# Half-row projections in one burst, the tails' first MLP layer with stationary weights, and a split last output group in a fused attention and gated-MLP kernel

## The chip, the cores and the metric

The kernel runs on one core of a Trainium2 chip. A core has a matrix engine (TensorE, PE in the profile, with its weight loads shown apart as PEld), three engines that work on tiles in on-chip memory (VectorE or DVE, ScalarE or ACT, GpSimd or POOL), and SyncE (SP), which here only issues transfers. Each engine runs its own instructions in order; semaphores join them. Matrix products land in PSUM, which has eight banks of 2 KB per partition; one bank holds 128 partitions by 512 float32 values. The metric is the device time of one launch in microseconds. The kernel before takes 278.93 us, the median of 13 runs from 277.47 to 279.93.

## The reference

Eight batches of eight heads, 576 tokens, head size 64, go through an attention with a feature map instead of a softmax, and the result through a gated MLP:

```python
def phi(x):                                  # x: q or k, w_phi: 64 x 128
    proj = einsum('bhsd,df->bhsf', x, w_phi)
    proj = proj - max(abs(proj), axis=-1)
    return concatenate([exp(proj), exp(-proj)], axis=-1)
q_p, k_p = phi(q), phi(k)
kv  = einsum('bhsf,bhsd->bhfd', k_p, v)
num = einsum('bhsf,bhfd->bhsd', q_p, kv)
den = einsum('bhsf,bhf->bhs', q_p, k_p.sum(axis=2)) + 1e-06
x = (num / den)                              # laid out as batch, token, 512

h = maximum(x @ w_in, 0)                     # 512 -> 1024
u, v = h[..., :512], h[..., 512:]
v_n = (v - mean(v)) / sqrt(var(v) + 1e-06)
v_s = einsum('ts,bsd->btd', w_spatial, v_n) + b_spatial
out = (u * v_s) @ w_out                      # 512 -> 512
```

## The kernel before, in words

The 576 tokens of a batch are cut into four blocks of 128 and a tail of 64. The attention works in *units*. A pair unit holds two heads of one batch with all four blocks, so eight slots of 128 tokens; a tail unit holds the tails of two neighbouring batches, all eight heads. There are 32 pair units and 4 tail units, 36 in all.

`step(i)` writes out one step of a software pipeline by hand. In each step the units near `i` pass their phases in the order of `ORDER`: keys, queries, attention, sums, next, features, out, maxima; a unit reaches the later phases some steps after the first ones (`LAGS`). The instructions stay on each engine in the order in which they are written. In the phase "keys" `a_keys` (L270) projects the keys: `by_token` (L263) fills one PSUM bank by two matmuls, each with 128 tokens of two heads as stationary operand (128 rows: 64 of one head, 64 of the other) and `wphi2`, a block-diagonal 128x256 copy of `w_phi`, as moving operand. So half the products are with zeros. DVE reduces the bank to the largest absolute value per token and head (L278), and ACT takes two exponentials of it (L281). `a_scale` then scales the values on POOL (L306). The phase "queries" does the same projection of the queries, of which only the maxima are taken (L292), split in a high and a low bfloat16 part (L295, L296), and turned by a PE transpose (`a_max_t`, L327). The phase "features" projects the queries a second time, by feature (L344, L348, L357), with the maxima subtracted by the same matmuls, and ACT takes exponentials (L365). "sums" forms `kv` (L378, L380), "attention" the quotient (L398, L388, L389).

Between the phases, `fill(share)` takes tasks of the MLP from `queue`. Each task has a cost in us of PE time (`MM` for four matmuls of 512 columns, `MS` for five). A step spends `share` of `rate` at each phase, at most `CAP` saved up, and a task is written out once the credit covers half its cost. `b_tasks(b)` (L604) lists the tasks of a batch: the first output groups of the batch before, `b_v_tail` (the v half of the first layer for the 64 tail tokens), four `b_v`, the norms, four `b_u`, `b_u_tail`, four `b_s` (the product with `w_spatial`), `b_s_tail`; the output groups `b_o` are mixed in. What is left when the units are done runs at the end, where `out_tasks(b)` of the last batch closes the kernel: four `b_o` and `b_o_tail`, each a product, a copy out of PSUM by DVE and ACT in turn (L564), and stores from the SP queue (L570, L576).

`b_v_tail` (L488) calls `v_mm` (L444): four matmuls whose stationary operand is `xTt`, 128 rows by 64 tail tokens, and whose moving operand is 512 columns of `w_in` (L447); then ACT's Relu (L449) and DVE's statistics (L450, L451). `b_u_tail` (L519) does the u half the other way round: sixteen matmuls with a 128x128 block of `w_in` stationary and the 64 tokens moving (L527), then one Relu (L529).

All PSUM tiles come from one pool of eight banks, `psum`, which is handed out in turn: a tile waits until the tile taken eight before it has been read. SBUF tiles have pools of their own with fixed numbers of buffers: `vr` five, `ob` six, `uTt` one.

Of the kernel before, what the change touches and what calls it, by code (L numbers as in the profile page):

```python
# [16 lines left out]
def kernel(  # L17
# [15 lines left out]
    nc = tc.nc  # L33
# [6 lines left out]
    P = 128  # L40
# [81 lines left out]

    wphi_f = cpool.tile([P, F], FP32)
    for i in range(2):
# [137 lines left out]

    def by_token(xT, half):  # L263
        ps = psum.tile([P, 4, F], FP32, tag="bank", name="ps")
        for x in range(2):
            nc.tensor.matmul(out=ps[:, 2 * x:2 * x + 2, :], lhsT=xT[:, 2 * half + x, :], rhs=wphi2,  # L266
                             start=True, stop=True)
        return ps

    def a_keys(u):  # L270

        u["mk"] = small.tile([P, H], FP32, tag="mk", name="mk")
        u["kf"] = feat.tile([P, 2, H, F], BF16, tag="kf" if u["pair"] else "kf_t", name="kf",
                            bufs=4 if u["pair"] else 2)
        for half in range(2):
            pk = by_token(u["kT"], half)
            hs = slice(4 * half, 4 * half + 4)
            nc.vector.tensor_reduce(out=u["mk"][:, hs], in_=pk, axis=AX.X, op=ALU.max,  # L278
                                    apply_absolute_value=True)
            for s, sc in ((0, 1.0), (1, -1.0)):  # L280
                nc.scalar.activation(out=u["kf"][:, s, hs, :], in_=pk, func=AF.Exp, bias=0.0, scale=sc)  # L281

    def a_queries(u):

        m, early = mhl[u["i"] % NM], u["i"] < EARLY
        if not early:
            mq = small.tile([P, H], FP32, tag="mq", name="mq")
        for half in range(2):
            pq = by_token(u["qT"], half)
            if early and half == 0:  # L290
                mq = pq[:, 0, 0:H]
            nc.vector.tensor_reduce(out=mq[:, 4 * half:4 * half + 4], in_=pq, axis=AX.X, op=ALU.max,  # L292
                                    apply_absolute_value=True)
        eng = nc.vector if early else nc.gpsimd
        eng.tensor_copy(out=m[:, 0:H], in_=mq)  # L295
        eng.tensor_tensor(out=m[:, H:2 * H], in0=mq, in1=m[:, 0:H], op=ALU.subtract)  # L296

# [211 lines left out]
    def b_u(b, dc):  # L509
# [7 lines left out]
        nc.scalar.activation(out=d["uT"][:, dc, :], in_=pu, func=AF.Relu, bias=0.0, scale=1.0)  # L517

    def b_u_tail(g, bls):  # L519
        d = gs[g]  # L520
        if bls[0] == 0:
            d["uTt"] = s2.tile([P, KC, P], BF16, tag="uTt", name="uTt", bufs=1)
        r = slice(bls[0] * TL, (bls[-1] + 1) * TL)
        pu = psum.tile([P, KC, P], FP32, tag="bank", name="pu")
        for dc in range(KC):
            for kc in range(KC):
                nc.tensor.matmul(out=pu[:, dc, r], lhsT=w_in_bf[:, kc, dc * P:(dc + 1) * P],  # L527
                                 rhs=d["xTt"][:, kc, r], start=(kc == 0), stop=(kc == KC - 1))
        nc.scalar.activation(out=d["uTt"][:, :, r], in_=pu[:, :, r], func=AF.Relu, bias=0.0, scale=1.0)  # L529

# [36 lines left out]
    def b_o(b, j):  # L567
        ob = o_mm(lambda dc: st[b]["uT"][:, dc, j * P:(j + 1) * P], slice(0, P))
        dst = bass.AP(tensor=out.tensor, offset=out.offset + b * S * DM + POS[j] * DM, ap=[[NB * DM, P], [1, DM]])
        nc.sync.dma_start(out=dst, in_=ob)  # L570

    def b_o_tail(g, bls):
        r = slice(bls[0] * TL, (bls[-1] + 1) * TL)
        ob = o_mm(lambda dc: gs[g]["uTt"][:, dc, r], r)
        for bl in bls:
            nc.sync.dma_start(out=out[2 * g + bl, T0:S, :], in_=ob[bl * TL:(bl + 1) * TL, :])  # L576
# [71 lines left out]
    def step(i):  # L648
# [120 lines left out]
```

## Time and profile before

| what | value |
|---|---|
| median of the runs | 278.93 us (13 runs, 277.47 to 279.93) |
| the profiled execution's own time | 279.18 us |
| its span, first to last instruction | 277.4 us |
| PE matmuls | 3047, busy 257.5 us (93%) |
| weight loads | 3047, busy 171.8 us (62%) |
| DVE | 614 instructions, busy 236.8 us (85%) |
| ACT | 501 instructions, busy 218.4 us (79%) |
| POOL | 312 instructions, busy 184.0 us (66%) |
| projections by token, L266 | 288 matmuls of 256 columns |
| units' keys phases | the first at 5.8 us, the last at 221.5 us; 28 of 36 start after 41 us |

A matmul's row in the profile has the time from its start until its result is out, and neighbours overlap; what a matmul takes of PE is the time from its start to the next one's start. A form such as 128\*64 128x512 names the rows and columns of the stationary operand that are in use and then the output's partitions and columns. Idle time of an engine is listed with what ended it. The span ends some us after the last store is issued, when its landing has been seen by SP and the engines have met.

### The profile page before, as it was taken

The page shows a single profiled execution, that of the slowest core. Times are in us where ns is not written, and L with a number is a line of the kernel's source. Part 1 is how long each engine was busy: PE and PEld are TensorE (multiplying, and loading weights), DVE is VectorE, ACT ScalarE, POOL GpSimd, SP SyncE. Part 2 cuts the span into 40 slices and gives each one's busy share as a digit, 9 for nine tenths or more (in the row PEclk, how much of TensorE's full clock was granted, in tenths as well). Part 3 has the DMA queues.
Part 4 walks back from the last instruction along what each step waited for, and adds up shares of the span by engine and source line. Part 5 has one row for each costly group of instructions (what it writes and reads, how often), then busy time and mean ns, then how long its engine had stood idle before and what let it go on. Part 6 is the DMA issues. An engine that isn't in the chain of part 4 may idle for free.

```text
span 277.4 us, 8178 instructions
## 1 busy us (share of the span) xinstructions
PE 257.5 (93%) x3047; PEld 171.8 (62%) x3047; DVE 236.8 (85%) x614; ACT 218.4 (79%) x501; POOL 184.0 (66%) x312
## 2 busy tenths in 40 slices
PE   3858999999999999999998999999998999999993
PEld 2547876767665676666765766667665765554441
DVE  7979998879999989998989989997998897565751
ACT  7898998797888978999898978998798977633511
POOL 4899899999579964898687954998448632410200
PEclk9999999999999999999999999999999999999998
DMA  7999999999999998999989999799854301211115
GB/s 194 201 258 131 158 157 94 158 224 209 184 188 190 231 217 134 224 177 221 132 112 192 258 188 151 167 225 165 140 90 122 87 2 58 94 42 40 76 40 189
DMA packets 84840, 42.43 MB, mean 153 GB/s; under 512 B 51840, under 2 KB 80192, under 8 KB 84800
## 3 DMA queue, kind: packets, MB, share of 16 engines
q1 hardware_dynamic: 60240, 30.95, 52.7%
q0 software_dynamic: 24400, 10.89, 36.9%
q8 instruction: 24, 0.39, 0.6%
q14 instruction: 16, 0.13, 0.2%
q10 hardware_dynamic: 160, 0.07, 0.1%
HBM read 32.85 MB, written 9.44 MB: 152 GB/s over the span
## 4 chain that ended last, share of the span: by engine, by line
PE 72%; ACT 11%; DVE 8%; POOL 3%; issue 2%; DMA 2%; SPq 0%; ACTq 0%
PE pv L447 10%; PE ps L536 10%; PE po L561 9%; PE pu L515 9%; PE ps L266 7%; ACT kf L281 6%; PE pv L378 5%; PE pn L398 4%; ACT qf L365 3%; PE pq L344 3%; PE ps L537 2%; DVE mk L278 2%; DMA first<-in_k_dram 2%; PE pn L426 2%; PE ps L548 1%
## 5 line engine op out<-in xcount | busy, mean ns | idle before, releaser
L306 POOL TENSOR_TENSOR vs<-v_f,em 128x512 bf16<-128x512 f32 x64 | 65.4, 1043 | 27.7 <-ACT em L301 25.2
L281 ACT ACTIVATE kf<-ps 128x512 bf16<-128x512 f32 x144 | 75.3, 633 | 7.4 <-DVE mk L278 7.4
L365 ACT ACTIVATE qf<-pq 128x512 bf16<-128x512 f32 x128 | 66.5, 621 | 10.2 <-PE pq L344 7.5
L278 DVE TENSOR_REDUCE mk<-ps 128x4 f32<-128x512 f32 x72 | 46.3, 681 | 1.0 <-PE ps L266 0.3
L292 DVE TENSOR_REDUCE mq<-ps 128x4 f32<-128x512 f32 x62 | 39.8, 678 | 2.1 <-PE ps L266 2.0
L561 PE MATMUL po<-w_out_bf,uT 128*128 128x512 bf16 x128 | 32.3, 379 | 1.0 <-ACT kf L281 0.8
L461 POOL TENSOR_TENSOR rs<-var,neghalf 64x1 f32<-64x1 f32 (+1 forms) x16 | 12.8, 799 | 30.5 <-DVE var L456 30.2
L536 PE MATMUL ps<-w_spT,vn 128*128 128x512 bf16 x128 | 33.0, 379 | 0.0
L450 DVE BATCH_NORM_STATS2 stats<-vr 128x6 f32<-128x512 bf16 (+1 forms) x40 | 26.7, 684 | 6.5 <-ACT vr L449 6.2
L515 PE MATMUL pu<-xT,w_in_bf 128*128 128x512 bf16 x128 | 32.1, 379 | 0.0
L447 PE MATMUL pv<-w_in_bf,xT 128*128 128x512 bf16 x128 | 31.4, 379 | 0.7 <-ACT kf L281 0.6
L449 ACT ACTIVATE vr<-pv 128x512 bf16<-128x512 f32 (+1 forms) x40 | 23.8, 618 | 8.8 <-PE pv L447 8.4
L539 DVE TENSOR_TENSOR uT<-ps,uT 128x512 bf16<-128x512 f32 x32 | 22.0, 687 | 8.5 <-PE ps L537 7.6
L378 PE MATMUL pv<-vs,kf 128*128 128x66 bf16 x512 | 24.5, 193 | 1.3 <-ACT kf L281 1.2
L389 DVE TENSOR_TENSOR x<-pn,rc 128x256 bf16<-128x256 f32 x64 | 25.0, 416 | 0.3
L398 PEld LDWEIGHTS <-qf 128*128 128x128 bf16 x512 | 20.2, 97 | 7.4 <-issue 1.7
L517 ACT ACTIVATE uT<-pu 128x512 bf16<-128x512 f32 x32 | 19.6, 640 | 6.3 <-PE pu L515 3.2
L378 PEld LDWEIGHTS <-kf 128*128 128x128 bf16 x512 | 21.7, 97 | 4.2 <-issue 3.5
L380 PE MATMUL pv<-vst,kf 128*128 128x66 bf16 x128 | 21.2, 191 | 1.9 <-POOL vst L61 1.9
L398 PE MATMUL pn<-kv,qf 128*128 128x66 bf16 x512 | 21.9, 193 | 0.9 <-ACT kf L281 0.3
L564 ACT COPY ob<-po 128x512 f32<-128x512 f32 x18 | 11.0, 612 | 14.3 <-PE po L561 8.8
L467 POOL TENSOR_SCALAR vn<-vr,rs 128x512 bf16<-128x512 bf16 x28 | 21.3, 769 | 0.9
(130 smaller groups left out, 564.2 us busy)
## 6 DMA issues: line engine op xcount, KB each, us to landing
out_dram<-ob SPq DMA_DIRECT2D x32, 256.0 KB, 2.9
v_f<-in_v_dram SPq DMA_DIRECT2D x14, 512.0 KB, 5.7
k_bf<-in_k_dram POOLq DMA_DIRECT2D x14, 256.0 KB, 6.5
q_bf<-in_q_dram POOLq DMA_DIRECT2D x14, 256.0 KB, 5.9
qt<-qT_b SPq DMA_DIRECT2D x24, 64.0 KB, 4.2
v_tl<-in_v_dram SPq DMA_DIRECT2D x8, 128.0 KB, 5.6
v_f<-in_v_dram SPq DMA_DIRECT2D x1, 1024.0 KB, 9.2
w_in_bf<-in_moe_w_in_dram POOLq DMA_DIRECT2D x2, 512.0 KB, 6.2
```

The lines of the kernel that those rows point to most:

```text
L278: nc.vector.tensor_reduce(out=u["mk"][:, hs], in_=pk, axis=AX.X, op=ALU.max, apply_absolute_value=True)
L281: nc.scalar.activation(out=u["kf"][:, s, hs, :], in_=pk, func=AF.Exp, bias=0.0, scale=sc)
L292: nc.vector.tensor_reduce(out=mq[:, 4 * half:4 * half + 4], in_=pq, axis=AX.X, op=ALU.max, apply_absolute_value=True)
L306: nc.gpsimd.tensor_tensor(out=vs[:, s, :, 0:D], in0=st[u["b"]]["v"][:, pj * H:(pj + 1) * H, :], in1=em[:, s, :].unsqueeze(2).to_broadcast( ...
L365: nc.scalar.activation(out=qf[:, s], in_=pq, func=AF.Exp, bias=0.0, scale=sc)
L378: nc.tensor.matmul(out=pv[:, hh, s, :], lhsT=u["kf"][:, s, 4 * hh + c, :], rhs=u["vs"][:, s, 4 * hh + c, :], start=(c == 0), stop=False)
L398: nc.tensor.matmul(out=pn[:, pos, :], lhsT=u["qf"][hh][:, s, pos, :], rhs=d["kv"][:, 2 * u["pj"] + hh, s, :], start=(s == 0), stop=(s == 1))
L447: nc.tensor.matmul(out=pv[r], lhsT=lhs(kc), rhs=w_in_bf[:, kc, HALF:DFF], start=(kc == 0), stop=(kc == KC - 1))
L450: nc.vector.bn_stats(out=stats[r], in_=dst[r])
L515: nc.tensor.matmul(out=pu, lhsT=w_in_bf[:, kc, dc * P:(dc + 1) * P], rhs=d["xT"][:, kc, :], start=(kc == 0), stop=(kc == KC - 1))
L536: nc.tensor.matmul(out=ps, lhsT=d["vn"][:, sp, cs], rhs=w_spT[:, sp, 0:T0], start=(sp == 0), stop=False)
L561: nc.tensor.matmul(out=po[r], lhsT=lhs(dc), rhs=w_out_bf[:, dc, :], start=(dc == 0), stop=(dc == KC - 1))
```

## The change

- `by_token` now takes a whole unit's keys or queries. For each of the four slots of two heads it issues two matmuls on half of the rows each: rows 0 to 63 (one head) against the first 128 columns of `wphi2`, rows 64 to 127 (the other head) against the last 128. The two heads' results go to two different PSUM banks. So 8 matmuls of 128 columns replace 4 of 256.
- `a_project`, new, does both keys and queries at the start of "keys": 16 matmuls in a row into four banks. The phase "queries" only reads.
- The banks now hold heads of one parity instead of four neighbouring heads; `mk`, `kf` and the two halves of `mhl` are written with a stride of two heads so that all that follows finds its order.
- `b_v_tail` forms both halves of the tail's first layer with `w_in` stationary and 64 tokens moving, 32 matmuls into one bank, and two Relus; `b_u_tail` is gone. `b_turn_tail`, new, runs two `b_v` later: four PE transposes of the v half, a DVE copy, and the statistics. Its cost in the queue is `MM / 4`.
- In the last batch the tail's output group runs second, and the last group, `b_o_last`, is done in two halves of 256 columns, copied by ACT and DVE and stored from ACT's and SP's queues.
- `wphi_f` moves from a buffer of its own into the ring `ob`; `uTt` gets two buffers; `vTt` shares the ring `vr`.

```diff
-    wphi_f = cpool.tile([P, F], FP32)
+    wphi_f = s2.tile([P, F], FP32, tag="ob", name="wphi_f", bufs=6)
...
-    def by_token(xT, half):
-        ps = psum.tile([P, 4, F], FP32, tag="bank", name="ps")
-        for x in range(2):
-            nc.tensor.matmul(out=ps[:, 2 * x:2 * x + 2, :], lhsT=xT[:, 2 * half + x, :], rhs=wphi2,
-                             start=True, stop=True)
+    def by_token(xT):
+        ps = [psum.tile([P, 4, F], FP32, tag="bank", name="ps") for _ in range(2)]
+        for j in range(4):
+            for y in range(2):
+                r = slice(y * D, (y + 1) * D)
+                nc.tensor.matmul(out=ps[y][:, j, :], lhsT=xT[r, j, :], rhs=wphi2[r, y * F:(y + 1) * F],
+                                 start=True, stop=True)
         return ps
+
+    def parity(t, y):
+        return t.rearrange("p (j two) -> p j two", two=2)[:, :, y]
+
+    def a_project(u):
+        u["pk"], u["pq"] = by_token(u["kT"]), by_token(u["qT"])
...
-        for half in range(2):
-            pk = by_token(u["kT"], half)
-            hs = slice(4 * half, 4 * half + 4)
-            nc.vector.tensor_reduce(out=u["mk"][:, hs], in_=pk, axis=AX.X, op=ALU.max,
+        for y, pk in enumerate(u["pk"]):
+            nc.vector.tensor_reduce(out=parity(u["mk"], y), in_=pk, axis=AX.X, op=ALU.max,
                                     apply_absolute_value=True)
             for s, sc in ((0, 1.0), (1, -1.0)):
-                nc.scalar.activation(out=u["kf"][:, s, hs, :], in_=pk, func=AF.Exp, bias=0.0, scale=sc)
+                nc.scalar.activation(out=u["kf"][:, s].rearrange("p (j two) f -> p j two f", two=2)[:, :, y, :],
+                                     in_=pk, func=AF.Exp, bias=0.0, scale=sc)
...
+        for y, pq in enumerate(u["pq"]):
+            nc.vector.tensor_reduce(out=mq[:, 4 * y:4 * y + 4], in_=pq, axis=AX.X, op=ALU.max, apply_absolute_value=True)
...
     def b_v_tail(g, bls):
         d = gs[g]
+        if bls[0] == 0:
+            d["uTt"] = s2.tile([P, KC, P], BF16, tag="uTt", name="uTt", bufs=2)
+        d["vTt"] = s2.tile([P, KC, TL], BF16, tag="vr", name="vTt", bufs=5)
         r = slice(bls[0] * TL, (bls[-1] + 1) * TL)
+        pu = psum.tile([P, 2 * KC, TL], FP32, tag="bank", name="pu")
+        for dc in range(2 * KC):
+            for kc in range(KC):
+                nc.tensor.matmul(out=pu[:, dc, :], lhsT=w_in_bf[:, kc, dc * P:(dc + 1) * P],
+                                 rhs=d["xTt"][:, kc, r], start=(kc == 0), stop=(kc == KC - 1))
+        nc.scalar.activation(out=d["vTt"], in_=pu[:, KC:2 * KC, :], func=AF.Relu, bias=0.0, scale=1.0)
+        nc.scalar.activation(out=d["uTt"][:, :, r], in_=pu[:, 0:KC, :], func=AF.Relu, bias=0.0, scale=1.0)
+
+    def b_turn_tail(g, bls):
+        d = gs[g]
+        r = slice(bls[0] * TL, (bls[-1] + 1) * TL)
+        pt = psum.tile([P, KC, P], BF16, tag="bank", name="pt")
+        for dc in range(KC):
+            nc.tensor.transpose(out=pt[r, dc, :], in_=d["vTt"][:, dc, :], identity=ident)
         vr = s2.tile([P, HALF], BF16, tag="vr", name="vr", bufs=5)
...
-        v_mm(lambda kc: d["xTt"][:, kc, r], vr, r, stats, mv[:, 0, :])
+        nc.vector.tensor_copy(out=vr[r], in_=pt[r].rearrange("p n e -> p (n e)"))
+        nc.vector.bn_stats(out=stats[r], in_=vr[r])
+        nc.vector.bn_aggr(out=mv[r, 0, :], in_=stats[r])
         d["ln"] = vr, moments(mv, r, 1)
...
+    def b_o_last(b, j):
+        dst = bass.AP(tensor=out.tensor, offset=out.offset + b * S * DM + POS[j] * DM, ap=[[NB * DM, P], [1, DM]])
+        for y, copy, queue_ in ((0, nc.scalar.copy, nc.scalar), (1, nc.vector.tensor_copy, nc.sync)):
+            n = slice(y * DM // 2, (y + 1) * DM // 2)
+            po = psum.tile([P, DM // 2], FP32, tag="bank", name="po")
+            for dc in range(KC):
+                nc.tensor.matmul(out=po, lhsT=st[b]["uT"][:, dc, j * P:(j + 1) * P], rhs=w_out_bf[:, dc, n],
+                                 start=(dc == 0), stop=(dc == KC - 1))
+            ob = s2.tile([P, DM], FP32, tag="ob", name="ob", bufs=6)
+            copy(out=ob[:, 0:DM // 2], in_=po)
+            queue_.dma_start(out=dst[:, n], in_=ob[:, 0:DM // 2])
...
+        if b == B - 1:
+            ts = ts[:1] + ts[-1:] + ts[1:NB - 1] + [(MM, lambda: b_o_last(b, NB - 1))]
...
-        ts = outs[:1] + [(MM, lambda: b_v_tail(g, [bl]))] + vs[:2] + outs[1:2] + vs[2:]
+        ts = outs[:1] + [(MM, lambda: b_v_tail(g, [bl]))] + vs[:2]
+        ts += [(MM / 4, lambda: b_turn_tail(g, [bl]))] + outs[1:2] + vs[2:]
...
-        ts += [(MM / 2, lambda: b_u_tail(g, [bl]))] + ss
+        ts += ss
...
                 if what == "keys":
+                    a_project(u)
                     a_keys(u)
```

More of the change, by code (lines that the diff above doesn't have):

```diff
@@ L274, in a_keys @@
                             bufs=4 if u["pair"] else 2)
-        for half in range(2):
-            pk = by_token(u["kT"], half)
-            hs = slice(4 * half, 4 * half + 4)
-            nc.vector.tensor_reduce(out=u["mk"][:, hs], in_=pk, axis=AX.X, op=ALU.max,
+        for y, pk in enumerate(u["pk"]):
+            nc.vector.tensor_reduce(out=parity(u["mk"], y), in_=pk, axis=AX.X, op=ALU.max,
                                     apply_absolute_value=True)
             for s, sc in ((0, 1.0), (1, -1.0)):
-                nc.scalar.activation(out=u["kf"][:, s, hs, :], in_=pk, func=AF.Exp, bias=0.0, scale=sc)
+                nc.scalar.activation(out=u["kf"][:, s].rearrange("p (j two) f -> p j two f", two=2)[:, :, y, :],
+                                     in_=pk, func=AF.Exp, bias=0.0, scale=sc)
     def a_queries(u):
         m, early = mhl[u["i"] % NM], u["i"] < EARLY
-        if not early:
+        if early:
+            mq = u["pq"][0][:, 0, 0:H]
+        else:
             mq = small.tile([P, H], FP32, tag="mq", name="mq")
[L288 to L293, printed above, removed]
+        for y, pq in enumerate(u["pq"]):
+            nc.vector.tensor_reduce(out=mq[:, 4 * y:4 * y + 4], in_=pq, axis=AX.X, op=ALU.max, apply_absolute_value=True)
         eng = nc.vector if early else nc.gpsimd
-        eng.tensor_copy(out=m[:, 0:H], in_=mq)
-        eng.tensor_tensor(out=m[:, H:2 * H], in0=mq, in1=m[:, 0:H], op=ALU.subtract)
+        hi, lo = (m[:, e * H:(e + 1) * H].rearrange("p (j two) -> p two j", two=2) for e in range(2))
+        mq = mq.rearrange("p (two j) -> p two j", two=2)
+        eng.tensor_copy(out=hi, in_=mq)
+        eng.tensor_tensor(out=lo, in0=mq, in1=hi, op=ALU.subtract)
     def a_scale(u):
@@ L517, in b_u @@
         nc.scalar.activation(out=d["uT"][:, dc, :], in_=pu, func=AF.Relu, bias=0.0, scale=1.0)
[L519 to L529, printed above, removed]
     def b_s(b, dc):
```

## The prediction

> **What bounds the kernel now.** I read the page's shares and slices first, then the busy time of two stretches, the waits, and last the timeline around the lines that change.
>
> ```profile
> PE 257.5 (93%) x3047; PEld 171.8 (62%) x3047; DVE 236.8 (85%) x614; ACT 218.4 (79%) x501; POOL 184.0 (66%) x312
> ...
> PE   3858999999999999999998999999998999999993
> ...
> DVE  7979998879999989998989989997998897565751
> ```
> ```profile
> 40.00:230.00 190.00, 185.76 (x2277) 125.75 (x2274) 173.42 (x441) 164.60 (x385) 142.78 (x245) 1.00 1.05 165
> 230.00:277.40 47.40, 42.86 (x374) 22.89 (x373) 27.13 (x72) 19.53 (x37) 7.72 (x13) 0.98 0.23 79
> ```
> ```profile
> DVE uT L539 <- PE ps L537: 4.2, 6, 1.0
> DVE qT_b L330 <- PE pt L327: 4.2, 6, 1.0
> DVE mq L292 <- PE ps L266: 2.0, 5, 0.7
> ```
>
> The second fence holds two stretches: length, then busy time (and instructions) of PE, PEld, DVE, ACT, POOL, then the granted clock, here 1.00. There are three stages. Up to 40 us PE has gaps and is not the bound. From 40 to 230 us PE is busy 185.8 of 190 us and DVE 173.4 (91%), so DVE has 16.6 us to spare; the third fence (waits in that stretch) shows that much of that slack is spent waiting for PE. After 230 us only PE is near full. So PE time saved after 40 us counts, until DVE has no slack.
>
> **The projections.** What the old ones take of PE is read from starts in the timeline, not from the rows' 273 ns:
>
> ```profile
> 120.47 0.60 PE L266 MATMUL ps<-wphi,kT_b 128*128 128x256 bf16 x4
> 120.91 1.03 PE L561 MATMUL po<-w_out_bf,uT 128*128 128x512 bf16 x4
> ```
> ```profile
> 53.88 0.40 PE L236 MATMUL pt<-ident,wsp 128*128 128x128 bf16 x4
> 54.21 0.20 PE L236 MATMUL pt<-ident,wspt 64*128 64x64 bf16 x1
> 54.34 0.41 PE L236 MATMUL pt<-ident,wsp 128*64 128x128 bf16 x8
> 54.68 0.22 PE L236 MATMUL pt<-ident,wspt 64*64 64x64 bf16 x2
> ```
> ```profile
> 133.39 0.28 PE L344 MATMUL pq<-qT_b,wm 128*128 128x128 bf16 x2
> 133.59 0.29 PE L439 MATMUL pt<-ident,xt 64*128 64x64 bf16 x4
> 133.81 0.23 PE L327 MATMUL pt<-ident,mhl 128*128 128x128 bf16 x1
> ```
>
> Four matmuls of 256 columns take 0.44 us, 0.109 each; a unit has eight: **0.872 us**. The new unit has sixteen of 128 columns on half the rows. Does a pair on different rows run together? No row of the trace has that. The nearest is L236 at 54.34, pairs on different *columns* of the array: eight matmuls in 0.34 us, and within it the starts come in pairs, 3 ns inside a pair and mostly 56 ns from pair to pair, which is what one 128-column matmul takes (the L344 rows at 133.39: 56 ns). Sixteen in eight pairs are then 8 x 56 = 0.45 us; the densest stream in the trace (L527 below) has 29 ns per load and matmul, 16 x 29 = **0.464**, which I take. The other end is no overlap: 16 x 56 = 0.90.
>
> Here a rule speaks against the change. The Trainium skill, "TensorEngine Tiling (Array Packing)", Key Properties, says that switching the tiling mode, not just the tile, drains TensorE. The last fence prices it. L439 works on 64 rows. From 133.39 two L344 take 0.11, so it could start at 133.50; it starts at 133.59. Its four take 0.12 (29 each), so L327 could start at 133.71; it starts at 133.81. Each way costs 0.095 us. Had I left the rule out, a unit would save 0.872 - 0.464 = 0.41; with it, in and out once per burst: 0.872 - 0.464 - 0.19 = **0.218 us per unit**. A second rule is harsher: "TensorE: Matmul & The Clock Gate", Back-to-back issue gap, gives about 81 ns sustained for a load and a 128-column matmul; sixteen one after another would be 1.3 us and the unit 0.61 slower. The L344 rows, each with its own load, take 56, so the trace decides against that figure.
>
> 28 units start after 41 us: 28 x 0.218 = 6.1 us. For the eight before I take nothing: from 20 to 40 us DVE is busy 19.3 of 20, and the first bank of keys is complete at 0.095 + 0.45 instead of 0.22, queries earlier than before; either sign stays under 0.5 us in all.
>
> **The tails' first layer**, eight times:
>
> ```profile
> 138.50 1.05 PE L447 MATMUL pv<-w_in_bf,xTt 128*64 128x512 bf16 x4
> 139.48 0.29 PE L344 MATMUL pq<-qt,wm 128*128 128x128 bf16 x2
> ```
> ```profile
> 262.91 0.63 PE L527 MATMUL pu<-xTt,w_in_bf 128*128 128x64 bf16 x16
> 263.37 0.38 PE L536 MATMUL ps<-w_spT,vn 128*128 128x512 bf16 x1
> ```
>
> Old v half: 0.98 us from start to start, the way out included, and 0.09 in: 1.07. New: sixteen with the weights stationary, as L527 has them, 0.46; then the four turns, 64 columns of the array, 4 x 56 and two switches, 0.41; 0.87 together. The u half is 0.46 before and after. Gain 0.2 x 8: 1.2 us in the middle stretch, 0.3 after it. ACT trades a Relu of 64x512 (593 ns) for one of 128x256 (461): 1 us less, not on the path. **DVE gains a copy** of 64x512 out of PSUM, nearest row L413 (128x512, 419 ns): 8 x 0.42 = 3.4 us, 2.5 of it before 230 us. The new wait is the turn on ACT's Relu. Two `b_v` (1.73 us) lie between; an ACT read of a `b_v` bank begins 0.3 us (median) to 1.8 us (one in ten) after PE is done, so rarely late; behind it would wait all of PE, and DVE's statistics. I take nothing, at most 0.3 us x 8.
>
> **The end.**
>
> ```profile
> 271.83 1.03 PE L561 MATMUL po<-w_out_bf,uTt 128*128 128x512 bf16 x4
> ...
> 272.94 0.59 ACT L564 COPY ob<-po 128x512 f32<-128x512 f32 x1 [1.14 <-PE po L561]
> 273.55 1.11 SPq L576 DMA_DIRECT2D out_dram<-ob  x2
> ```
>
> Now: copy 0.59, then two stores; the second issues at 274.07. New: the last half's DVE copy is 128x256, 0.42 by L389, so one SP store issues near 272.95 + 0.42 = 273.37. ACT's half finishes 0.44 us earlier on PE and its store goes from ACT's own queue. The tail's two stores go before. Landing as now: **0.7 us** off. A slower landing from ACT's queue could take it all back.
>
> **Edits at nothing.** `wphi_f` in `ob`: with four `first` and `wspt` it makes six tiles in six buffers, all read long before the first output copy at 75 us. `vTt` in `vr`: the sixth tile takes its buffer, free after the turn. The strides of two heads keep runs of 128 elements. POOL's 31 pairs of L295/L296 keep their sizes. SP keeps its transfers and has one store more at the end, off its queue.
>
> **What takes some back: the banks.** PSUM tiles take the eight banks in turn. I paired every tile in the trace with its last reader. In the 27 units from 48 us on, the tiles taken 4, 3 and 2 before a keys phase are free 0.61, 1.29 and 1.99 us after its start (median), 0.90, 1.66 and 2.58 in the slowest tenth; two of them are the features' banks, read by ACT for 2.06 us:
>
> ```profile
> 139.99 0.60 PE L266 MATMUL ps<-wphi,kT_b 128*128 128x256 bf16 x4
> 140.20 2.06 ACT L365 ACTIVATE qf<-pq 128x512 bf16<-128x512 f32 x4
> ```
>
> The burst takes four banks at once. The next tile comes at 0.65 us (0.095 + 0.464 + 0.095), those behind it at 1.51 and 2.4 with tasks of 0.86: spare 0.04, 0.22 and 0.4 us in the median, short by about 0.2 in the slow tenth. Before, the queries' two banks were asked for only after one or two tasks. Price: 0 to 0.25 us per unit; I take 0.1, near the median: 28 x 0.1 = 2.8 us. This is also how a busier DVE and ACT would hold PE back, so I don't charge DVE again.
>
> **Sum.** Middle: 6.1 + 1.2 - 2.8 = 4.5 us. DVE there: (173.4 + 2.5) of 185.5 us, 95%; from 20 to 40 us it ran at 97%, so it can. Later: 0.3 + 0.7 = 1.0. In all **5.5 us off the span of 277.4: 271.9**. That execution took 279.18 and the median is 278.93; I take the difference from the median: **273.4 us**.
>
> **Rivals.**
> - *All of it arrives.* The burst hands DVE and ACT their work sooner, and the three waits shown above (10.4 us) shrink with PE. No bank stall: 8.3 us off, 270.6. Against it: DVE would be at 175.9 of 182.7, 96%.
> - *DVE and the banks become the bound.* A stall of 0.26 us per unit, the slow tenth everywhere, eats 7.3 us: only the end is left, 277.9; with DVE's 2.5 us uncovered, 280.4. For it: ACT's 2 us of features at each keys phase. Against it: PE waited only some 4 us for readers in this stretch.
> - *The row halves do not overlap* (slower). Place: the burst. 0.90 + 0.19 - 0.872 = +0.214 us per unit, x 28 = +6.0; tails and end give 2.2 back: +3.8, **282.7**. It decides once sixteen matmuls take more than 0.68 us, 43 ns each, before the rest. For it: no pair on rows stands in the trace. Against it: the pairs on columns do overlap, and the two row halves here go to different banks.
>
> **How the numbers follow.** Chances: partial gain 0.45 (own range 271 to 276), all of it 0.20, DVE and banks 0.18, no overlap 0.13, else 0.04. Within 0.2% (0.56 us) is about what a measurement here cannot tell from no change. Faster: 0.45 + 0.20 + 0.07 of the third + 0.01 = 0.73; same 0.06; slower 0.13 + the rest = 0.21. The range 269.8 to 280.6 holds the first two and most of the third case, and leaves the no-overlap case above it.
>
> **What would show it.** Right: matmuls on 64 rows starting in pairs a few ns apart, a burst near 0.46 us with about 0.095 before and behind; PE's busy share still over 95% from 40 to 225 us; DVE near 95% there; few PE waits on L365's and the keys' readers; last SP issue followed by the same landing. Wrong: starts 56 ns apart in the burst; PE waiting for ACT right behind the burst by more than 0.2 us per unit; PE held at the turn; DVE without idle time while PE has gaps.

## The result, and the profile after

The changed kernel takes 281.29 us (median of 11 runs, 280.08 to 282.27) against 278.89 us (48 runs, 277.43 to 280.13): the ratio is 1.009, with a 95% interval of 1.0072 to 1.0107. It is 2.4 us slower, where 5.5 us faster was forecast (273.4 us), and it lies 0.7 us above the top of the stated range, 280.6 us. Its profiled execution took 280.58 us. Below, differences in us are the ratio's distance from 1, times 278.9 us.

The page of the changed kernel, shares and slices:

```profile
span 278.8 us, 9013 instructions
...
PE 252.9 (91%) x3467; PEld 166.8 (60%) x3467; DVE 239.1 (86%) x623; ACT 216.7 (78%) x501; POOL 184.2 (66%) x312
...
PE   3787899899996999999997999999987999999993
...
DVE  7989998969999899998899898997999897565752
```

PE's busy time fell by 4.6 us, and the span still grew by 1.4 us. From the seventh of the 40 slices on (after 40 us) PE's row has slices of 6, 7 and 8; before, all of these but the last were 8 or 9.

The same two stretches as before, length first, then busy time of PE, PEld, DVE, ACT and POOL:

```profile
40.00:230.00 190.00, 179.94 (x2589) 119.59 (x2588) 173.17 (x441) 161.90 (x382) 141.66 (x243) 1.00 1.03 164
230.00:278.80 48.80, 43.63 (x407) 23.89 (x402) 28.59 (x77) 19.46 (x38) 7.71 (x13) 0.98 0.22 77
```

From 40 to 230 us PE is idle for 10.1 us; before it was 4.2. DVE is busy for 173.2 us, as before (173.4): in the same 190 us it did no more than it had done, though the kernel now asks more of it.

The waits of that stretch (who waited, for what: us, times, longest):

```profile
ACT kf L287 <- DVE mk L284: 10.7, 15, 2.3
...
DVE qT_b L337 <- PE pt L334: 4.4, 5, 1.2
...
PE pv L385 <- ACT kf L287: 3.4, 5, 1.4
...
PE ps L268 <- DVE x L396: 2.1, 4, 0.8
...
DVE uT L553 <- PE ps L551: 1.7, 4, 0.4
```

DVE's wait for the product with `w_spatial` (then 4.2 us) has shrunk. What has grown is the chain from DVE to ACT to PE: ACT's exponentials of the keys wait 10.7 us for the key maxima (before 5.0), and PE's sums wait 3.4 us for ACT (before 1.2). A new one is PE's burst waiting for DVE to empty a bank. In the chain of work that ended last, PE had 72% and DVE 8% before; the page of the changed kernel has

```profile
PE 49%; DVE 23%; ACT 10%; DMA 6%; issue 4%; POOL 3%; SPq 3%; POOLq 0%; ACTq 0%
```

These shares alone do not tell a slower kernel from a faster one: the projections alone, which lose nothing, have PE 47% and DVE 18%, and the fastest version below that still computes the reference has PE 46% and DVE 20%.

The timeline around one burst of the changed kernel (start, duration, engine, and what it does):

```profile
127.03 0.22 PE L334 MATMUL pt<-ident,mhl 128*128 128x128 bf16 x1
127.18 0.40 PE L268 MATMUL ps<-wphi,kT_b 64*128 64x128 bf16 x8
127.42 0.39 PE L268 MATMUL ps<-wphi,qT_b 64*128 64x128 bf16 x8
...
127.73 1.04 PE L550 MATMUL ps<-w_spT,vn 128*128 128x512 bf16 x4
```

L334 takes 0.056 us, so PE is free at 127.09 and the burst starts at 127.18: about 0.095 us to switch in. The next matmul starts 0.55 us after the burst began: the burst's 0.46 and about 0.09 to switch out. Inside, starts are 3 to 4 ns apart in a pair and 56 ns from pair to pair. So what the burst itself costs came out as forecast. Another burst did not go so well, in the timeline of the same kernel:

```profile
85.00 0.40 PE L268 MATMUL ps<-wphi,kT_b 64*128 64x128 bf16 x8
85.37 0.38 PE L268 MATMUL ps<-wphi,qT_b 64*128 64x128 bf16 x4
86.11 0.41 DVE L396 TENSOR_TENSOR x<-pn,rc 128x256 bf16<-128x256 f32 x1
86.57 0.38 PE L268 MATMUL ps<-wphi,qT_b 64*128 64x128 bf16 x4 [0.82 <-DVE x L396]
...
88.90 1.29 DVE L284 TENSOR_REDUCE mk<-ps 128x4 f32<-128x512 f32 x2
89.62 2.06 ACT L287 ACTIVATE kf<-ps 128x512 bf16<-128x512 f32 x4 [2.35 <-DVE mk L284]
...
90.76 0.29 PE L385 MATMUL pv<-vs,kf 128*128 128x66 bf16 x4 [1.42 <-ACT kf L287]
```

The burst stops in its middle for 0.82 us, because the bank it needs next still holds what DVE reads at 86.11. Its keys are complete by 85.4, but DVE takes their maxima only at 88.9: until then it works without a gap at what stands ahead in its queue (two blocks' statistics, the quotients, two copies). ACT waits 2.35 us and PE 1.42 us. A faster burst is worth nothing here.

### The profile page after: what moved, and what is told of

Read it like the earlier page. It is cut to its first block, busy times and chain, and to the rows that moved or that the text cites. A ratio compares the mean times of both kernels' runs of the same rounds, so it can differ in the third digit from the quotient of the medians.

```text
span 278.8 us, 9013 instructions
## 1 busy us (share of the span) xinstructions
PE 252.9 (91%) x3467; PEld 166.8 (60%) x3467; DVE 239.1 (86%) x623; ACT 216.7 (78%) x501; POOL 184.2 (66%) x312
## 4 chain that ended last, share of the span: by engine, by line
PE 49%; DVE 23%; ACT 10%; DMA 6%; issue 4%; POOL 3%; SPq 3%; POOLq 0%; ACTq 0%
PE ps L550 8%; PE po L575 7%; PE pu L541 7%; ACT kf L287 6%; PE pv L454 5%; DVE mk L284 4%; DVE stats L457 3%; PE pv L385 3%; PE ps L268 3%; SPq L61 3%; PE pn L405 3%; DMA qT_b<-q_bf 3%; DVE x L396 2%; PE pu L504 2%; PE pq L351 2%
## 5 line engine op out<-in xcount | busy, mean ns | idle before, releaser
L298 DVE TENSOR_REDUCE mq<-ps 128x4 f32<-128x512 f32 x62 | 40.5, 678 | 0.2
L541 PE MATMUL pu<-xT,w_in_bf 128*128 128x512 bf16 x128 | 31.4, 379 | 0.0
L457 DVE BATCH_NORM_STATS2 stats<-vr 128x6 f32<-128x512 bf16 x32 | 21.5, 682 | 8.4 <-ACT vr L456 8.3
L396 DVE TENSOR_TENSOR x<-pn,rc 128x256 bf16<-128x256 f32 x64 | 25.0, 416 | 0.4
L456 ACT ACTIVATE vr<-pv 128x512 bf16<-128x512 f32 x32 | 19.5, 623 | 4.8 <-PE pv L454 4.5
L578 ACT COPY ob<-po 128x512 f32<-128x512 f32 x17 | 10.2, 603 | 16.4 <-PE po L575 16.2
```

Of the source, the lines that this page charges most:

```text
L298: nc.vector.tensor_reduce(out=mq[:, 4 * y:4 * y + 4], in_=pq, axis=AX.X, op=ALU.max, apply_absolute_value=True)
L396: nc.vector.tensor_tensor(out=x, in0=pn[r, :, 0:D], in1=rc[r].to_broadcast([n, 4, D]), op=ALU.mult)
L541: nc.tensor.matmul(out=pu, lhsT=w_in_bf[:, kc, dc * P:(dc + 1) * P], rhs=d["xT"][:, kc, :], start=(kc == 0), stop=(kc == KC - 1))
```

## The experiments

Each ratio is against the kernel before, timed on the same chip. The first four experiments take the change apart.

**The projections alone.**

```diff
-            pk = by_token(u["kT"], half)
...
+    def a_project(u):
+        u["pk"], u["pq"] = by_token(u["kT"]), by_token(u["qT"])
...
+        for y, pk in enumerate(u["pk"]):
```

> The projections alone: half rows, keys and queries in one burst; tails and last group as before. Theory A (the burst asks for four banks at once, while DVE and ACT are behind, and PE stands where it used to run a task): slower than before, by 1 to 3 us (280 to 282). Theory B (the extra DVE copy and the turn of the tails cost the time, the burst is a gain): faster by 1 to 4 us (275 to 278).

Measured: 278.94 us, ratio 0.9998 [0.9974, 1.0022]. Neither theory forecast it: no gain and no loss. The stretch of 40 to 230 us in this kernel:

```profile
40.00:230.00 190.00, 180.48 (x2471) 117.65 (x2502) 173.00 (x441) 164.98 (x387) 143.01 (x245) 1.00 1.09 166
```

By its busy time PE has 5.3 us less to do than before (180.5 against 185.8), and what it saved has become idle time. The 5.3 is somewhat too high: the trace has 2471 matmuls of this stretch for 2502 weight loads, so 31 records are missing. DVE, ACT and POOL have got through as much as before (441, 387 and 245 instructions, then 441, 385 and 245).

**The tails' first layer alone.**

```diff
-        v_mm(lambda kc: d["xTt"][:, kc, r], vr, r, stats, mv[:, 0, :])
...
+        for dc in range(2 * KC):
+            for kc in range(KC):
+                nc.tensor.matmul(out=pu[:, dc, :], lhsT=w_in_bf[:, kc, dc * P:(dc + 1) * P],
+                                 rhs=d["xTt"][:, kc, r], start=(kc == 0), stop=(kc == KC - 1))
...
+        ts += [(MM / 4, lambda: b_turn_tail(g, [bl]))] + outs[1:2] + vs[2:]
```

> The tails' change alone: first layer with stationary weights, v turned back. Theory A: within 0.7 us of before. Theory B: slower by 2 to 4 us (281 to 283), with DVE late in the stretches of the v tasks and about 0.8 us lost before the last w_spatial products.

Measured: 282.27 us, ratio 1.0133 [1.0101, 1.0164], +3.7 us, as theory B forecast. The loss is here. In this kernel's waits the same one has grown, from 5.0 to 9.1 us:

```profile
ACT kf L281 <- DVE mk L278: 9.1, 8, 2.4
```

**The last group alone.**

```diff
+        for y, copy, queue_ in ((0, nc.scalar.copy, nc.scalar), (1, nc.vector.tensor_copy, nc.sync)):
...
+        if b == B - 1:
+            ts = ts[:1] + ts[-1:] + ts[1:NB - 1] + [(MM, lambda: b_o_last(b, NB - 1))]
```

> The last output group alone in two halves, tail's group second. Both theories: 0.2 to 0.7 us faster (the profiles before and after put the time from PE's end to the span's end at 4.5 and 4.3 us).

Measured: 278.76 us, ratio 0.9995 [0.998, 1.0011]. No difference that can be told, where both theories looked for 0.2 to 0.7 us.

**Half rows, but the queries' projection left in its own phase** (two banks at a time, two more mode switches per unit).

```diff
     def a_project(u):
-        u["pk"], u["pq"] = by_token(u["kT"]), by_token(u["qT"])
+        u["pk"] = by_token(u["kT"])
...
+        u["pq"] = by_token(u["qT"])
```

> Half rows, but the queries projected in their own phase as before, so two banks at a time; tails and last group as before. PE then pays the mode switch four times a unit: 0.872 - 0.464 - 0.38 = 0.03 us saved per unit, 1 us in all at most. Theory A: 0 to 1 us faster than before, so 2 to 3 us faster than the projections in one burst. Theory B: 0 to 1 us faster than before, and slower than the burst by 1 to 4 us.

Measured: 279.20 us, 1.0019 [0.9997, 1.0041]. That is level with the burst within the intervals; both theories looked for 0 to 1 us faster than before.

The three parts alone add up to +3.5 us, the whole to +2.5. The next four look at what each costs by itself.

**The burst with the old full rows.**

```diff
+    def a_project(u):
+        u["pk"] = [by_token(u["kT"], half) for half in range(2)]
+        u["pq"] = [by_token(u["qT"], half) for half in range(2)]
```

> The burst without the half rows: keys and queries of a unit in one go, 8 matmuls of 256 columns on full rows, four banks at once; no mode switch, PE's work as before. Theory A2 (four banks taken at once hold PE back, and that eats the 6 us that the half rows save): slower than before by 3 to 6 us (282 to 285). Theory C (the steady stage is paced by DVE, ACT and the banks together, so that PE's saving just turns into PE's idle time): within 1 us of before.

Measured: 279.93 us, 1.0047 [1.0028, 1.0066]. Neither forecast is met. The burst by itself costs 1.3 us. That its hold on four banks is the reason is not shown: from 40 to 230 us PE is busy 185.4 us in this run (185.8 before), and its listed waits there add up to 3.7 us (3.6 before). Half rows, given the burst, are worth 0.9998 / 1.0047, about 1.4 us.

**The tails' change with the turned half copied by ACT.**

```diff
-        nc.vector.tensor_copy(out=vr[r], in_=pt[r].rearrange("p n e -> p (n e)"))
+        nc.scalar.copy(out=vr[r], in_=pt[r].rearrange("p n e -> p (n e)"))
```

> The tails' change alone, but the turned v half is copied out of PSUM by ACT instead of DVE (8 copies of 64x512). If DVE's 3.4 us more are what the tails cost: 2 to 3 us faster than the tails' change with DVE's copy (279 to 280.5). If the turn's place or the moved u half costs: within 1 us of it (281.5 to 283).

Measured: 281.22 us, 1.0083 [1.005, 1.0115]: +2.3 us, where the copy on DVE gave +3.7. Moving the copy off DVE is worth 1.4 us, less than half of the loss. The result lies between the two forecasts, and the intervals of the two runs overlap a little.

**The v half turned, the u half left in its old task.**

```diff
-        ts += ss
+        ts += [(MM / 2, lambda: b_u_tail(g, [bl]))] + ss
```

> The tails' v half with stationary weights and turned back, but the u half in its old task behind the b_u. If the v half's turn and copy cost the time: as slow as the tails' change (281.5 to 283). If the moved u half costs: 279 to 280.

Measured: 286.43 us (283.01 to 287.03), 1.0243 [1.0198, 1.0288]: +6.8 us, more than either forecast. The size is not clean: the two runs at a granted clock of 1.00 took 283.0 and 284.0 us, the four at 0.98 to 0.99 took 286.4 to 287.0. But none is as low as the 282.27 us of the tails' change, so the u half's move is no part of the loss.

**The u half moved, the v half as before.**

```diff
         v_mm(lambda kc: d["xTt"][:, kc, r], vr, r, stats, mv[:, 0, :])
+        b_u_tail(g, bls)
...
-        ts += [(MM / 2, lambda: b_u_tail(g, [bl]))] + ss
+        ts += ss
```

> The v half as before (four matmuls of 512 columns, no turn), only the u half moved up into the v task. If the moved u half costs: 281 to 283. If the turn and its copy cost: within 1 us of before (278 to 280).

Measured: 277.64 us, 0.9958 [0.9939, 0.9977]: 1.2 us faster than before, better than both forecasts. (The edit also gives `uTt` the second buffer that the early place needs.) From here to the tails' change is 1.0133 / 0.9958 = 1.0176, 4.9 us, for all that turning the v half brings: the turn, the copy and the later statistics.

The next four ask how much DVE's load matters at all.

**Before, with one more DVE pass over each tail's v half.**

```diff
+        if more:
+            nc.vector.tensor_scalar(out=dst[r], in0=dst[r], scalar1=0.0, scalar2=None, op0=ALU.max)
         nc.vector.bn_stats(out=stats[r], in_=dst[r])
```

> The kernel before with one more DVE pass over each tail's v half (64x512, in place, the larger of the value and 0, which changes nothing) ahead of its statistics, eight in all, 0.2 to 0.42 us each by the row that it will have; PE and ACT as before. Theory D (in the stretches of the v and u tasks DVE sets the pace, so DVE work there costs its own length and PE's saving there is worth nothing): slower than before by about the added time, 1.6 to 3.4 us. Rival (DVE has slack, the turn's wait is what the tails cost): within 0.6 us.

Measured: 280.11 us, 1.0049 [1.0027, 1.0071]: +1.4 us. The group's row in this kernel (busy us, mean ns):

```profile
L451 DVE TENSOR_SCALAR vr<-vr 64x512 bf16<-64x512 bf16 x8 | 3.4, 430 | 3.4 <-ACT vr L449 3.2
```

By this row it adds 3.4 us to DVE, about as much as the copy does (DVE's busy time on the page rises by less, from 236.8 to 238.4 us), and 1.4 us reach the end, just under the least that theory D forecast. That is the size by which the ACT copy is better.

**Before, with the block statistics over 256 of 512 columns.**

```diff
-        nc.vector.bn_stats(out=stats[r], in_=dst[r])
+        nc.vector.bn_stats(out=stats[r], in_=dst[r, 0:HALF // 2])
```

> The kernel before with the statistics of v taken over 256 of the 512 columns (40 times about 0.33 us of DVE less, 13 us in all); the output is then not the reference's. Theory D: faster than before by 3 to 8 us, with PE then without gaps. If PE alone is the bound: within 1 us.

Measured: 275.88 us, 0.9896 [0.9875, 0.9917]: 2.9 us faster, for 8.5 us less of DVE's busy time (228.3 on the page, 236.8 before). That is just short of theory D's 3 to 8 us.

**The projections' change with those lighter statistics.** The edit is the one above, in the kernel with the projections alone.

> The projections on half rows in one burst, again with the statistics over half the columns (output not the reference's). Theory D: now that DVE is relieved, PE's 0.218 us per unit count, and it is 3 to 6 us faster than the kernel before with the same lighter statistics. If the burst's hold on the banks eats the saving: within 1 us of it.

Measured: 274.13 us, 0.9837 [0.9812, 0.9862]. Against the lighter kernel before it is 0.9837 / 0.9896 = 0.994, so 1.7 us. With DVE relieved the projections are worth something, but not the 3 us and more that I looked for. Both made lighter give 4.5 us (0.9837), DVE alone 2.9 and PE alone nothing. The stretch in the two lighter kernels, the old projections first:

```profile
40.00:230.00 190.00, 188.17 (x2320) 127.64 (x2319) 169.32 (x451) 165.75 (x388) 143.22 (x248) 1.00 1.07 167
```
```profile
40.00:230.00 190.00, 185.39 (x2565) 120.51 (x2563) 169.31 (x453) 167.34 (x392) 144.00 (x248) 1.00 1.11 167
```

With DVE lighter, PE is idle for 1.8 us instead of 4.2. The new projections bring the idle time back to 4.6.

**The change with the tails' v half undone** (u half early, half rows in a burst, the split end stay).

```diff
-        ts += [(MM / 4, lambda: b_turn_tail(g, [bl]))] + outs[1:2] + vs[2:]
+        ts = outs[:1] + [(MM, lambda: b_v_tail(g, [bl]))] + vs[:2] + outs[1:2] + vs[2:]
...
+        v_mm(lambda kc: d["xTt"][:, kc, r], vr, r, stats, mv[:, 0, :])
+        b_u_tail(g, bls)
```

> The changed kernel with the tails' v half undone (four matmuls of 512 columns, no turn, no DVE copy), all else as changed: half rows in one burst, the u half moved up into the v task, last group in halves. Theory D: 1 to 2 us faster than before (277 to 278), that is 3 to 4.5 us faster than the changed kernel. If the parts hinder each other in another way: not faster than before.

Measured: 276.06 us, 0.991 [0.9876, 0.9944]: 2.5 us faster than before, 5.1 us faster than the change (1.009 / 0.991 = 1.0182), somewhat more than forecast. One step undone turns the sign.

The copy on DVE accounts for about 1.4 of these 5 us. The turn also puts the tails' statistics two `b_v` later in DVE's queue, since they now follow the turn. The next three runs test that place (S) against the turn's wait (W).

**Before, with only the tails' statistics two `b_v` later.** No turn, no copy, no work added.

```diff
-        v_mm(lambda kc: d["xTt"][:, kc, r], vr, r, stats, mv[:, 0, :])
...
+    def b_stats_tail(g, bls):
...
+        nc.vector.bn_stats(out=stats[r], in_=vr[r])
+        nc.vector.bn_aggr(out=mv[r, 0, :], in_=stats[r])
...
+        ts += [(0.0, lambda: b_stats_tail(g, [bl]))] + outs[1:2] + vs[2:]
```

> The kernel before with one thing moved: the tails' statistics (DVE, 0.68 + 0.17 + 0.28 us, eight times) come two v tasks later, where the changed kernel has them; no turn, no copy, no other work. Theory S (the turn moves DVE's tail work out of the seam behind the w_spatial tasks, where DVE has slack, into the v tasks, where it has none, and delays all DVE work behind it): slower than before by 1 to 3 us. Theory W (PE's wait at the turn, or the turn's own matmuls and mode switches, cost the time): within 0.6 us.

Measured: 282.88 us, 1.0157 [1.0131, 1.0182]: +4.4 us, more than the 1 to 3 us of theory S. What moves is about 1.1 us of DVE's work per batch: the tail's statistics of 0.68 us and the three short operations that follow from them. Moving this, and nothing else, costs more than the whole change. One batch in the two timelines, before first:

```profile
111.39 0.59 ACT L449 ACTIVATE vr<-pv 64x512 bf16<-64x512 f32 x1
...
112.02 0.69 DVE L450 BATCH_NORM_STATS2 stats<-vr 64x6 f32<-64x512 bf16 x1
...
113.73 1.27 DVE L450 BATCH_NORM_STATS2 stats<-vr 128x6 f32<-128x512 bf16 x2
...
115.94 1.29 DVE L278 TENSOR_REDUCE mk<-ps 128x4 f32<-128x512 f32 x2
...
121.73 1.27 DVE L278 TENSOR_REDUCE mk<-ps 128x4 f32<-128x512 f32 x2
```

and with the statistics late:

```profile
111.36 0.59 ACT L498 ACTIVATE vr<-pv 64x512 bf16<-64x512 f32 x1
...
113.14 0.69 DVE L450 BATCH_NORM_STATS2 stats<-vr 128x6 f32<-128x512 bf16 x1 [0.34 <-ACT vr L449]
...
114.62 0.67 DVE L505 BATCH_NORM_STATS2 stats<-vr 64x6 f32<-64x512 bf16 x1
...
116.37 1.27 DVE L278 TENSOR_REDUCE mk<-ps 128x4 f32<-128x512 f32 x2
...
122.30 1.27 DVE L278 TENSOR_REDUCE mk<-ps 128x4 f32<-128x512 f32 x2
```

The Relu ends at the same time. In the kernel before, DVE takes the tail's statistics at once, at 112.02. In the other it has nothing ready just then and waits (the 0.34 us in brackets); the tail's statistics come at 114.62, among work that is ready, and push it back. The next key maxima start 0.43 us late, those after them 0.57 us late. In the next batch the price is higher (DVE's rows, before first):

```profile
140.64 0.69 DVE L450 BATCH_NORM_STATS2 stats<-vr 64x6 f32<-64x512 bf16 x1
...
149.81 1.28 DVE L278 TENSOR_REDUCE mk<-ps 128x4 f32<-128x512 f32 x2
```
```profile
146.83 0.69 DVE L505 BATCH_NORM_STATS2 stats<-vr 64x6 f32<-64x512 bf16 x1
...
151.37 1.28 DVE L278 TENSOR_REDUCE mk<-ps 128x4 f32<-128x512 f32 x2
```

From the late statistics to these maxima DVE works without a gap, and the maxima start 1.56 us late; the unit before had its maxima 0.17 us early (141.59 against 141.76 us). The last unit's maxima are 2.8 us late (225.53 against 222.72). The waits of this kernel from 40 to 230 us show what hangs on them:

```profile
ACT kf L281 <- DVE mk L278: 7.0, 9, 2.0
...
DVE stats L450 <- ACT vr L449: 4.4, 8, 1.4
...
PE pv L378 <- ACT kf L281: 1.7, 2, 1.6
```

Before, they were 5.0, 1.3 and 1.2 us. The middle one is DVE's wait for a Relu ahead of the blocks' statistics: the gap that the tail's statistics had kept short. PE's idle time there is 6.1 us (before 4.2), which is about half of what this profiled execution lost: its span is 280.8 us, 3.4 more. All its lost granted clock lies before 40 us (1.00 from there on), and another run of this kernel, at 1.00, took 283.02 us, so the clock is not what made it slower.

**The turn one `b_v` earlier,** in the kernel with the tails' change alone.

```diff
-        ts = outs[:1] + [(MM, lambda: b_v_tail(g, [bl]))] + vs[:2]
-        ts += [(MM / 4, lambda: b_turn_tail(g, [bl]))] + outs[1:2] + vs[2:]
+        ts = outs[:1] + [(MM, lambda: b_v_tail(g, [bl]))] + vs[:1]
+        ts += [(MM / 4, lambda: b_turn_tail(g, [bl]))] + vs[1:2] + outs[1:2] + vs[2:]
```

> The tails' change alone with the turn one v task earlier (behind the first instead of the second). Theory S: 1 to 2 us faster than with the turn behind the second (280.3 to 281.3). Theory W: slower, since PE comes to the turn 0.86 us sooner and ACT's Relu is not done: 282.5 to 284.

Measured: 281.96 us, 1.0137 [1.0107, 1.0168], the same as two later. Both theories miss: S looked for 1 to 2 us better, W for at least 0.5 us more. The waits of this run, over its whole span, show something of both:

```profile
DVE vr L511 <- PE pt L507: 6.4, 5, 2.6
...
PE pt L507 <- ACT vTt L499: 1.0, 1, 1.0
```

With the turn behind the second `b_v`, DVE's wait for the turn (L511 is the copy) was 0.4 us and PE's wait for the Relu did not occur. So one `b_v` earlier DVE, which works in order, stands idle ahead of the copies. What the earlier place gives and what this wait takes were not timed apart.

**The turn behind all four `b_v`.**

```diff
+        ts = outs[:1] + [(MM, lambda: b_v_tail(g, [bl]))] + vs[:2] + outs[1:2] + vs[2:]
+        ts += [(MM / 4, lambda: b_turn_tail(g, [bl]))]
```

> The tails' change alone with the turn behind all four v tasks. Theory S: no faster than behind the second, 281.5 to 284, since the DVE work comes later still. Theory W: PE never waits at the turn there, 279.5 to 281.

Measured: 286.62 us, 1.0271 [1.0238, 1.0304]: +7.6 us, twice as much (284.5 to 287.1) and more than either theory allowed. More time between Relu and turn makes it worse. That the turn's wait for ACT is not the cost, behind the second `b_v`, is also in the trace of the tails' change; the last figure is PE's idle time ahead of the turns:

```profile
L507 PE MATMUL pt<-ident,vTt 128*64 128x128 bf16 x32 | 3.3, 225 | 0.0
```

The run with the turn behind all four is no pure test of DVE's queue, though. The tail's norm is the first that POOL takes: POOL's wait for DVE's moments is 37.0 us here and 29.0 in the tails' change, and PE's idle time ahead of the products with `w_spatial` is 2.5 us against 1.2. Later is worse or the same, never better.

**The early u half, charged with the extra MM/2 in the queue.**

```diff
-        ts = outs[:1] + [(MM, lambda: b_v_tail(g, [bl]))] + vs[:2] + outs[1:2] + vs[2:]
+        ts = outs[:1] + [(MM * 1.5, lambda: b_v_tail(g, [bl]))] + vs[:2] + outs[1:2] + vs[2:]
```

> The u half in the v task, as in the run that was 1.2 us faster than before, but with its half MM charged to the task's cost. If that gain came from the uncharged cost (more tasks written out between the units, fewer left for the end): the gain goes, within 0.5 us of before. If it came from the u half's place: 277.2 to 278.

Measured: 277.53 us, 0.9947 [0.9927, 0.9966]. So the gain of the early u half is due to its place (with the second buffer) and not to its task being missing from the queue's account.

The last two look at what the rest of the change is worth around that.

**The early u half with the split last group,** old projections.

```diff
+        b_u_tail(g, bls)
...
+            ts = ts[:1] + ts[-1:] + ts[1:NB - 1] + [(MM, lambda: b_o_last(b, NB - 1))]
```

> The kernel before with the u half in the v task and the last group in halves, projections as before. If the half-row burst has a value of its own once the v half is undone: slower than the changed kernel without the v half (0.991 of before) by 0.5 to 1.5 us, 0.995 of before. If it has none: equal to it.

Measured: 277.76 us, 0.9958 [0.9939, 0.9977]. The split group again adds nothing.

**The change with the v half undone, its task charged MM x 1.5.** The edit is that of the charged u half.

> The changed kernel without the tails' v half, and with half an MM more charged for the v task, which now does the u half as well. The uncharged cost made no difference in the kernel before, so within 0.7 us of the same without the charge: 0.988 to 0.994 of before.

Measured: 276.11 us, 0.9906 [0.9884, 0.9928], the same as without the charge. Against the kernel with the early u half and the split group, the projections are worth 0.991 / 0.9958 = 0.9952 without the charge and 0.9906 / 0.9958 = 0.9948 with it, so 1.3 to 1.5 us. This version, with or without the charge, beats both kernels. Its stretch from 40 to 230 us (without the charge):

```profile
40.00:230.00 190.00, 184.43 (x2547) 118.93 (x2546) 173.73 (x445) 165.29 (x387) 142.84 (x246) 1.00 1.08 166
```

DVE is busy for 173.7 us, as in nearly every version (173.0 to 173.7 in the kernels before, after, with the projections, with the tails' change; 170.6 with the statistics late). It looks as if the versions differ in how much of the kernel fits into that DVE time.

## Why the prediction was wrong, step by step

In the prediction's own terms, as us of gain: the projections less the price of the banks, 3.3 forecast and 0.0 measured; the tails, 1.5 forecast and -3.7 measured; the end, 0.7 forecast and 0.1 measured.

- **The bound.** "So PE time saved after 40 us counts, until DVE has no slack" failed. PE at 186 of 190 us and DVE at 173 looked like a PE bound with 16.6 us of slack on DVE. But DVE's gaps are not free for use. Two experiments show the load: 8.5 us less on DVE gave 2.9 us, and eight passes more cost 1.4, without any change to PE. And PE's saving of at most 5.3 us gave none of it (projections alone). PE made lighter gave nothing, DVE 2.9 us, both together 4.5. That fits two engines that set the pace together. The sign named for being right, DVE near 95% in this stretch, did not come: it stayed at 91%.
- **The burst's own time.** Right: row halves overlap in pairs, 0.46 us, about 0.095 to switch in and 0.09 out. The rival in which they do not overlap is out.
- **The projections' 6.1 us.** The saving in PE time is there (at most 5.3 us in 190). In time it is worth 0 alone, 1.7 with lighter statistics, 1.3 to 1.5 with the v half undone; the half rows without the burst's own cost are worth 1.4.
- **The banks' 2.8 us.** The size was too large: the burst with full rows costs 1.3 us, and its trace does not show that PE waits for banks, so the mechanism stays unproven. In the changed kernel PE does wait 2.1 us at the burst for DVE (L396). I let this price stand for a busier DVE as well, and that was wrong.
- **The tails.** A gain of 1.5 us was forecast, a loss of 3.7 measured. Two steps failed. "I don't charge DVE again": the copy, counted rightly (3.4 us forecast, 3.3 measured on DVE), cost 1.4. And the larger one is missing: the turn moves the tail's statistics behind two `b_v` in DVE's queue. I named them only as waiting behind the turn, and priced the wait of PE. The move alone costs 4.4 us in the kernel before. Together with the copy that is 5.8, against 4.9 for the v half's turn as a whole; the difference of 0.9 lies within the intervals, so what PE's saving gave back cannot be told.
- **The turn's wait.** "I take nothing, at most 0.3 us x 8" was right for this place: PE's idle time ahead of the turns is 0.0. One `b_v` earlier DVE would have waited 6.4 us for them.
- **The u half's place.** Taken as even, since its 0.46 us are the same before and after. Moving it is worth 1.2 us, which hides part of the v half's loss in the tails' change. Why the early place is better is not traced.
- **The end's 0.7 us.** From PE's last matmul to the end of the span it was 4.55 us, and it is 4.29 with the last group alone: 0.26 of gain, and 0.1 in time (interval 0.6 gain to 0.3 loss). The end of the changed kernel:

```profile
273.48 1.04 PE L592 MATMUL po<-w_out_bf,uT 128*128 128x256 bf16 x8
274.17 0.37 ACT L595 COPY ob<-po 128x256 f32<-128x256 f32 x1 [0.76 <-PE po L592]
274.56 0.42 DVE L595 COPY ob<-po 128x256 f32<-128x256 f32 x1 [0.18 <-PE po L592]
274.57 0.36 ACTq L596 DMA_DIRECT2D out_dram<-ob  x1
275.02 0.41 SPq L596 DMA_DIRECT2D out_dram<-ob  x1
```

  The copies and issues went as forecast: DVE's 0.42 us, and one store from each queue. But the landings were seen 3.1 and 2.9 us after the issue; before it was 2.4. The "slower landing" that I had named, for ACT's queue alone, took about 0.5 of the 0.7, from SP's queue as from ACT's. Why it is slower is not shown: the store of whole rows just ahead of these two, issued by SP at 274.52 us, took 3.0 us as well.
- **The rivals.** The second, DVE and the banks becoming the bound, was the right one in kind as far as DVE goes. Its worst value, 280.4, was too low, as it too moved no statistics. Within it only that upper end was slower than before, so the sign had too little chance.

**What stays open.** That the place of the statistics costs 4.4 us is shown in the kernel before; beside the turn it was not timed by itself. How 1.1 us of moved DVE work per batch comes to cost 0.5 us per batch on average is traced in two batches only, and half of the loss appears as idle time on PE. Nor do I know why the turned v half with the u half in its old place is, if anything, slower still than with it moved. The projections gain nothing alone and 1.3 to 1.5 us beside the early u half; with intervals of about 1 us that difference is only just clear, and its cause is open.

## What to carry to other kernels

A share of 98% on one engine and 91% on another, coupled by a few buffers and both in order, was not a bound with slack here: measure what each is worth by lightening it before pricing a saving at its full size. When an edit delays an operation, ask which gap its old place filled and what ready work it now stands in front of; here a move that adds no work cost 4.4 us, more than any part of the change gained. Of a change in several parts, time each alone and the whole without it: here one part of one part had the wrong sign, and the kernel without it beats both.

## What the runs showed of the hardware

- Matmuls of 128 columns on rows 0 to 63 and 64 to 127 into two banks start 3 to 4 ns apart in a pair and 56 ns from pair to pair, so two take the time of one. Going from full rows to half rows costs about 0.095 us, and back about 0.09.
- DVE's statistics take as long on 64 partitions (681 ns) as on 128 (682 ns) over 512 columns, and 417 ns over 256 columns. So a tail costs DVE what a full block does.
- The two half-row stores at the end (256 columns each) were seen to land 2.9 and 3.1 us after their issue, against 2.4 us for the last store before; a whole-row store issued just ahead of them took 3.0 us, so the shorter rows are not shown to be the reason.
